# Four batches per attention step, block products in the second MLP matmul, crossbar transposes and list-scheduled engines in a fused retention and MLP kernel

## The chip, the cores and the metric

The kernel runs on one core of one Trainium2 chip. The metric is device time in microseconds (us) of one execution. Each execution was graded fast or slow; on one core slow means over 1.5% above the fastest execution of the same kernel. The medians and ranges quoted hold every execution.

Engine names: PE is the matrix engine (TensorE), PEld its weight load, DVE is VectorE, ACT ScalarE, POOL GpSimd, SP the sequencer that issues most DMAs. "L403" is line 403 of the kernel file, so line numbers belong to one kernel.

## The reference, cut to what matters

```python
# attention: 8 batches, 8 heads, 576 positions, 64 columns a head, no softmax
scores = (1 / 8) * q @ k.transpose                 # per batch and head
gamma  = 1 - 2 ** (-5 - h)
Dmat   = where(i >= j, gamma ** (i - j), 0)
attn   = (scores * Dmat) @ v
x      = attn as (4608 tokens, 512)
# MLP
h = x @ w_in                                       # 512 -> 2048
g = h * cos(h)
out = g @ w_out                                    # 2048 -> 512
```

Both kernels factor the decay into q and v, and work through each sequence in nine chunks of 64 positions with a running 64x64 state per batch and head. The MLP runs in nine blocks of 512 tokens.

Of the kernel before, what the change touches and what calls it, by code (L numbers as in the profile page):

```python
# [14 lines left out]
CH = 64  # L15
NR = S // CH
NST = (B // 2) * NR
# [5 lines left out]
class Op:  # L23
    __slots__ = ("eng", "fn", "deps", "need", "val", "sem", "snap")
# [6 lines left out]
class Prog:  # L31
# [28 lines left out]
    def emit(self):  # L60
# [13 lines left out]
        for op in self.ops:  # L74
# [14 lines left out]
            inst = op.fn(self.handle[op.eng])  # L89
            op.snap = dict(mine)  # L90
# [11 lines left out]

class Kernel:
    def __init__(self, nc, es, q, k, v, w_in, w_out, out):
# [5 lines left out]
        self.NSTG, self.NNAT, self.NKT, self.NQ, self.NPT, self.NSB, self.NCB, self.NOS = 8, 5, 3, 3, 2, 2, 3, 4  # L110
        self.XT = sb("xt", [128, NST * 512], BF16)
        self.WIN = sb("win", [128, 4 * DFF], BF16)
        self.WOUT = sb("wout", [128, NF * DM], BF16)
        self.STG = [sb(f"stg{i}", [128, 2 * DM], F32) for i in range(self.NSTG)]
        self.NAT = [sb(f"nat{i}", [128, 2 * DM], BF16) for i in range(self.NNAT)]
        self.KT = [sb(f"kt{i}", [128, DM], BF16) for i in range(self.NKT)]
        self.QSTG = [sb(f"qstg{i}", [128, 2 * DM], F32) for i in range(self.NQ)]
        self.QNAT = [sb(f"qnat{i}", [128, 2 * DM], BF16) for i in range(self.NQ)]
        self.QT = [sb(f"qt{i}", [128, 2 * DM], BF16) for i in range(self.NQ)]
        self.PT = [sb(f"pt{i}", [128, 512], BF16) for i in range(self.NPT)]  # L120
        self.SBD = [sb(f"sbd{i}", [128, 512], BF16) for i in range(self.NSB)]
        self.GT = [sb(f"gt{i}", [128, NF * TB], BF16) for i in range(2)]
        self.CB = [sb(f"cb{i}", [128, TB], BF16) for i in range(self.NCB)]
        self.OS = [sb(f"os{i}", [128, DM], F32) for i in range(self.NOS)]
# [5 lines left out]
        self.DUM = sb("dum", [128, 512], BF16)  # L130
# [6 lines left out]
        self.SC = nc.alloc_psum_tensor("sc", [128, 1024], F32)  # L137
        self.ST = nc.alloc_psum_tensor("st", [128, 512], F32)
        self.BK = [nc.alloc_psum_tensor(f"bk{i}", [128, 512], F32) for i in range(5)]
        self.held, self.turn = {0}, 0  # L140
        self.n_cb = self.n_os = 0

    def build(self):
        self.constants()
        self.schedule()
        last = self.P.emit()
        for name, val in last.items():
            if name.startswith("o"):
                self.nc.sync.wait_ge(self.P.sems[name], val)


    def constants(self):
        P = self.P
        lng = [math.log(1.0 - 2.0 ** (-5.0 - h)) for h in range(H)]
        P.add("pool", lambda e: e.iota(self.IV.ap(), [[64, 9], [0, 8]], base=0, channel_multiplier=1,
# [4 lines left out]
                                       channel_multiplier=1, allow_small_or_imprecise_dtypes=True), w=["iqx"])  # L160
        for t, key, off, n, sub in ((self.IV, "iv", 0, 72, 64), (self.IQ, "iq", 0, 64, 128),
                                    (self.IQ, "iqx", 64, 8, 64)):
            P.add("dve", lambda e, t=t, off=off, n=n, sub=sub: e.tensor_scalar(
                ap(t, 72, 64, 64, off, [1, n]), ap(t, 72, 64, 64, off, [1, n]), float(sub), None, ALU.subtract),
                r=[key], w=[key])
        P.add("dve", lambda e: e.memset(self.ONE.ap(), 1.0), w=["one"])
        P.add("dve", lambda e: e.memset(self.DUM.ap(), 0.0), w=["dum"])
        for h in range(H):
            P.add("dve", lambda e, h=h: e.memset(ap(self.LV, 72, 0, 128, h, [8, 9]), -lng[h]), w=[("lv", h)])
            P.add("dve", lambda e, h=h: e.memset(ap(self.LQ, 72, 0, 128, h, [8, 9]), lng[h]), w=[("lq", h)])  # L170
        P.add("dve", lambda e: e.memset(self.CLN.ap(), math.log(1.0 / 8.0)), w=["cln"])
        P.add("dve", lambda e: e.memset(self.CPI.ap(), math.pi / 2), w=["cpi"])
# [7 lines left out]
        P.add("pool", lambda e: e.affine_select(self.IDN.ap(), self.ONE.ap(), pattern=[[1, 128]],  # L180
                                                compare_op=ALU.is_equal, fill=0.0, base=0,
                                                channel_multiplier=-1), r=["one"], w=["idn"])
# [12 lines left out]
    def load_kv(self, g, i, gate=()):  # L195
        p, r = g // NR, g % NR
        slot = g % self.NSTG
        for s in range(2):
            self.P.add("sp", lambda e, s=s: e.dma_start(  # L199
                ap(self.STG[slot], 2 * DM, 64 * s, 64, i * DM, [D, H], [1, D]),  # L200
                bass.AP(self.src[1 + i], ((2 * p + s) * H * S + CH * r) * D, [[D, CH], [S * D, H], [1, D]])),
                r=list(gate), w=[("stg", slot, i, s)], sem=f"i{slot}_{i}_{s}")

    def load_q(self, d, gate=()):
        p, r = d // 5, d % 5
        slot, m = d % self.NQ, (2 if d % 5 < 4 else 1) * D
        for s in range(2):
            self.P.add("sp", lambda e, s=s: e.dma_start(
                ap(self.QSTG[slot], 2 * DM, 64 * s, 64, 0, [m, H], [1, m]),
                bass.AP(self.src[0], ((2 * p + s) * H * S + 128 * r) * D, [[m, 64], [S * D, H], [1, m]])),  # L210
                r=list(gate), w=[("qstg", slot, s)], sem=f"q{slot}_{s}")

    def load_win(self, s, gate=()):
        self.P.add("pool", lambda e: e.dma_start(
            ap(self.WIN, 4 * DFF, 0, 128, s * 512, [DFF, 4], [1, 512]),
            bass.AP(self.w_in, s * 512, [[DFF, 128], [128 * DFF, 4], [1, 512]])),
            r=list(gate), w=[("win", s)], sem=f"wi{s}")

    def load_wout(self, s, gate=()):
        self.P.add("pool", lambda e: e.dma_start(  # L220
            ap(self.WOUT, NF * DM, 0, 128, s * 4 * DM, [DM, 4], [1, DM]),
            bass.AP(self.w_out, s * 4 * 128 * DM, [[DM, 128], [128 * DM, 4], [1, DM]])),
            r=list(gate), w=[("wout", s)], sem=f"wo{s}")


    def copy(self, eng, dst, src, r, w):
        if eng == "act":
            self.P.add(eng, lambda e: e.activation(dst, src, AF.Copy), r=r, w=w)  # L228
        else:
            self.P.add(eng, lambda e: e.tensor_copy(dst, src), r=r, w=w)  # L230

    def cast_k(self, g, eng):
        st, na = g % self.NSTG, g % self.NNAT
        self.copy(eng, ap(self.NAT[na], 2 * DM, 0, 128, 0, [1, DM]), ap(self.STG[st], 2 * DM, 0, 128, 0, [1, DM]),
                  [("stg", st, 0, 0), ("stg", st, 0, 1)], [("nat", na, 0)])

    def cast_v(self, g, eng):
        r, st, na = g % NR, g % self.NSTG, g % self.NNAT
        self.P.add(eng, lambda e: e.tensor_tensor(  # L239
            ap(self.NAT[na], 2 * DM, 0, 128, DM, [D, H], [1, D]),  # L240
            ap(self.STG[st], 2 * DM, 0, 128, DM, [D, H], [1, D]),
            ap(self.WV, 72, 0, 128, 8 * r, [1, H], [0, D]), ALU.mult),
            r=[("stg", st, 1, 0), ("stg", st, 1, 1), "wv"], w=[("nat", na, 1)])

    def cast_q(self, d, engs):
        r, k = d % 5, d % self.NQ
        for x, eng in enumerate(engs[:2 if r < 4 else 1]):
            step = 2 * D if r < 4 else D
            self.P.add(eng, lambda e, x=x, step=step: e.tensor_tensor(  # L249
                ap(self.QNAT[k], 2 * DM, 0, 128, x * DM, [D, H], [1, D]),  # L250
                ap(self.QSTG[k], 2 * DM, 0, 128, x * D, [step, H], [1, D]),
                ap(self.WQ, 72, 0, 128, 16 * r + 8 * x, [1, H], [0, D]), ALU.mult),
                r=[("qstg", k, 0), ("qstg", k, 1), "wq"], w=[("qnat", k, x)])

    def bank(self, hold=False):
        while self.turn % 5 in self.held:
            self.turn += 1
        i = self.turn % 5
        self.turn += 1
        if hold:  # L260
            self.held.add(i)
        return i, self.BK[i], ("bk", i)

    def step_tk(self, g, eng="act"):
        k = g % self.NNAT
        i, ps, key = self.bank()
        tb = ps.ap().bitcast(BF16)

        def mm(e):
            for c in range(4):  # L270
                inst = e.transpose(tb[:, c * 128:c * 128 + 128], ap(self.NAT[k], 2 * DM, 0, 128, 128 * c, [1, 128]),  # L271
                                   self.IDN.ap())
            return inst
# [66 lines left out]
    def session(self, g):  # L340
        r = g % NR
        now, nxt = 0 <= g, g + 1 < NST
        if now:
            i, ob, key = self.bank()
# [258 lines left out]
```

## The kernel before: what the change and the argument touch

An attention step covers one chunk of two batches (36 steps). Its small matmuls are 64x64, two batches side by side on the partitions. Keys and queries are transposed on PE against an identity, and evacuated by ACT:

```python
def step_tk(self, g, eng="act"):
    [...]
    for c in range(4):
        inst = e.transpose(tb[:, c*128:c*128+128], ap(self.NAT[k], ..., 128*c, [1,128]), self.IDN.ap())
    self.P.add("pe", mm, r=[("nat", k, 0), "idn"], w=[key])
    self.copy(eng, self.KT[t].ap(), tb[:, 0:512], [key], [("kt", t)])
```

The second MLP matmul is plain: for each 128 tokens, sixteen 512-column matmuls accumulate in one PSUM bank. Program order, per engine, is written by hand: after each few MLP pieces an attention piece is interleaved.

```python
def schedule(self):
    [...]
    for x in range(4):
        self.load_wout(x)
    at["cast"] = 4
    load_to(8, [("wout", 2)])      # the loads of steps 4 to 7 wait for three quarters of w_out
    cast_to(6)
    self.mlp1(0, 2, 0)
    T(4)                           # transposes of step 4: need the gated loads
    self.session(3)
    for f in (1, 2, 3):
        self.mlp1(0, 2, f)
    [...]
    for j in range(1, NTB):
        mlp = []
        for i in range(16):
            mlp.append(m1(4*(j+1), 4*(j+2), i))
            mlp.append(m2(j, i//4, i%4, ...))
        run(mlp, att_of(4*(j+2), 4*(j+3)))
```

## Time and profile before

| | before |
|---|---|
| time, median of 2 runs | 394.2 us (393.95 to 394.46) |
| span of the profiled run | 389.8 us |
| PE busy | 322.7 us, 83% |
| block of 512 tokens with attention | 35.5 us |
| hole on PE near the start | 25.5 to 48.6 us |
| last matmul to the end | 11.3 us |

The first view is the page of the kernel before. The first two lines are the span and the busy time by engine. The rows of digits cut the span into 40 slices; each digit is a busy share in tenths (9 is 90% or more), and PEclk is the granted clock of PE in tenths of full speed. Then come the instruction queue and the chain of waits by engine.

```profile
span 389.8 us, 8844 instructions
...
PE 322.7 (83%) x3695; PEld 172.4 (44%) x3728; DVE 130.3 (33%) x233; ACT 199.1 (51%) x331; POOL 96.1 (25%) x120
...
PE   5640089989777999899899989998998999999980
...
PEclk9555559999988999999999999999999999999995
DMA  8999992154469935363434444554321011001112
...
q8 instruction: 29, 0.48, 0.5%
...
PE 72%; DMA 10%; SPq 6%; ACT 4%; POOL 2%; issue 2%; DVE 0%; DVEq 0%; ACTq 0%; POOLq 0%
```

PE is the bound: it is busy in nearly every slice from the sixth on, and 72% of the chain of waits lies on it. The two zeros in the PE row are the hole. PE's timeline around the hole (start, duration, engine, line, operation, tiles, count; in brackets the idle time before it and what ended it):

```profile
24.50 1.04 PE L403 MATMUL bk<-xt,win 128*128 128x256 bf16 x4
48.59 1.03 PE L288 MATMUL bk<-idn,qnat 128*128 128x128 bf16 x8 [23.06 <-POOL qnat L249]
```

The first four matmuls of block 0 run at 24.50, and then PE sits for 23 us behind the transposes of step 4, whose query cast waits for a load that is gated on w_out.

### The profile page before, as it was taken

The page shows a single profiled execution, that of the slowest core. Times are in us where ns is not written, and L with a number is a line of the kernel's source. Part 1 is how long each engine was busy: PE and PEld are TensorE (multiplying, and loading weights), DVE is VectorE, ACT ScalarE, POOL GpSimd, SP SyncE. Part 2 cuts the span into 40 slices and gives each one's busy share as a digit, 9 for nine tenths or more (in the row PEclk, how much of TensorE's full clock was granted, in tenths as well). Part 3 has the DMA queues.
Part 4 walks back from the last instruction along what each step waited for, and adds up shares of the span by engine and source line. Part 5 has one row for each costly group of instructions (what it writes and reads, how often), then busy time and mean ns, then how long its engine had stood idle before and what let it go on. Part 6 is the DMA issues. An engine that isn't in the chain of part 4 may idle for free.

```text
span 389.8 us, 8844 instructions
## 1 busy us (share of the span) xinstructions
PE 322.7 (83%) x3695; PEld 172.4 (44%) x3728; DVE 130.3 (33%) x233; ACT 199.1 (51%) x331; POOL 96.1 (25%) x120
## 2 busy tenths in 40 slices
PE   5640089989777999899899989998998999999980
PEld 2420064547544545445454545454554454444450
DVE  3410027115532334244333334333343344243100
ACT  3350057349664566556655656655656555444220
POOL 2450273031327431313233323131312000000000
PEclk9555559999988999999999999999999999999995
DMA  8999992154469935363434444554321011001112
GB/s 157 167 190 202 201 208 38 41 136 108 127 161 197 202 98 132 97 176 101 101 97 122 122 122 101 148 138 118 90 80 31 29 33 50 21 31 35 41 46 70
DMA packets 106439, 42.51 MB, mean 109 GB/s; under 512 B 81184, under 2 KB 101920, under 8 KB 106400
## 3 DMA queue, kind: packets, MB, share of 16 engines
q1 hardware_dynamic: 102176, 37.76, 41.7%
q0 software_dynamic: 4224, 4.19, 6.6%
q8 instruction: 29, 0.48, 0.5%
q14 instruction: 10, 0.08, 0.1%
HBM read 36.70 MB, written 9.44 MB: 118 GB/s over the span
## 4 chain that ended last, share of the span: by engine, by line
PE 72%; DMA 10%; SPq 6%; ACT 4%; POOL 2%; issue 2%; DVE 0%; DVEq 0%; ACTq 0%; POOLq 0%
PE bk L403 31%; PE bk L427 29%; SPq L199 4%; DMA wout<-in_moe_w_out_dram 4%; PE bk L334 4%; PE bk L326 3%; DMA qstg<-in_q_dram 2%; DMA out_dram<-os 2%; PE bk L288 2%; PE bk L271 2%; ACT sbd L228 1%; ACT xt L228 1%; PE sc L308 1%; DMA stg<-in_k_dram 1%; POOL qnat L249 1%
## 5 line engine op out<-in xcount | busy, mean ns | idle before, releaser
L413 DVE TENSOR_TENSOR gt<-bk,cb 128x512 bf16<-128x512 f32 (+1 forms) x164 | 102.2, 627 | 179.8 <-ACT cb L410 175.0
L403 PE MATMUL bk<-xt,win 128*128 128x512 bf16 (+1 forms) x656 | 150.3, 363 | 10.5 <-ACT xt L228 10.3
L410 ACT ACTIVATE cb<-bk,cpi 128x512 bf16<-128x512 f32 (+1 forms) x164 | 103.0, 637 | 79.6 <-PE bk L403 79.5
L427 PE MATMUL bk<-wout,gt 128*128 128x512 bf16 (+1 forms) x561 | 137.3, 373 | 2.4 <-ACT os L441 0.7
L403 PEld LDWEIGHTS bk<-xt,win 128*128 128x128 bf16 x656 | 61.8, 101 | 64.1 <-ACT xt L228 11.2
L427 PEld LDWEIGHTS bk<-wout,gt 128*128 128x128 bf16 x592 | 57.4, 98 | 66.9 <-ACT os L441 2.1
L230 POOL CAST nat<-stg 128x512 bf16<-128x512 f32 x32 | 19.5, 610 | 172.6 <-PE st L316 102.3
L239 POOL TENSOR_TENSOR nat<-stg,wv 128x512 bf16<-128x512 f32 x36 | 37.5, 1042 | 13.0 <-DMA stg<-in_v_dram 12.7
L376 DVE TENSOR_TENSOR pt<-sc,tri 128x512 bf16<-128x512 f32 x36 | 24.6, 683 | 46.0 <-PE sc L308 46.0
L288 PE MATMUL bk<-idn,qnat 128*128 128x128 bf16 x144 | 12.5, 233 | 29.2 <-POOL qnat L249 26.4
L249 POOL TENSOR_TENSOR qnat<-qstg,wq 128x512 bf16<-128x512 f32 x32 | 32.8, 1041 | 11.4 <-DMA qstg<-in_q_dram 11.4
L228 ACT ACTIVATE qt<-bk 128x1024 bf16<-128x1024 bf16 (+1 forms) x18 | 16.7, 928 | 33.4 <-PE bk L288 33.4
L441 ACT ACTIVATE os<-bk 128x512 f32<-128x512 f32 (+1 forms) x37 | 21.7, 585 | 22.3 <-PE bk L427 22.3
L228 ACT ACTIVATE sbd<-st 128x512 bf16<-128x512 f32 x32 | 19.1, 598 | 23.5 <-PE st L316 23.5
L228 ACT ACTIVATE kt<-bk 128x512 bf16<-128x512 bf16 x36 | 21.4, 594 | 12.0 <-PE bk L271 12.0
L334 PE MATMUL bk<-pt,nat 64*64 64x64 bf16 x576 | 23.6, 204 | 3.2 <-PE st L316 0.5
L288 PEld LDWEIGHTS bk<-idn,qnat 128*128 128x128 bf16 x144 | 10.0, 104 | 33.8 <-POOL qnat L249 27.4
L228 ACT ACTIVATE xt<-bk 128x512 bf16<-128x512 f32 x36 | 21.4, 594 | 2.3 <-PE bk L334 2.3
L308 PE MATMUL sc<-qt,kt 64*64 64x64 bf16 x576 | 20.6, 204 | 1.5 <-DVE qt L230 0.8
L316 PE MATMUL st<-nat 64*64 64x64 bf16 x512 | 21.1, 205 | 0.0
L334 PEld LDWEIGHTS bk<-pt,nat 64*64 64x64 bf16 x576 | 15.5, 113 | 8.6 <-PE st L316 6.4
L326 PEld LDWEIGHTS bk<-qt,sbd 64*64 64x64 bf16 x512 | 11.4, 115 | 15.5 <-ACT cb L410 10.3
(36 smaller groups left out, 98.8 us busy)
## 6 DMA issues: line engine op xcount, KB each, us to landing
stg<-in_k_dram SPq DMA_DIRECT2D x72, 128.0 KB, 7.3
stg<-in_v_dram SPq DMA_DIRECT2D x72, 128.0 KB, 4.7
out_dram<-os SPq DMA_DIRECT2D x70, 128.0 KB
qstg<-in_q_dram SPq DMA_DIRECT2D x32, 256.0 KB, 5.9
win<-in_moe_w_in_dram POOLq DMA_DIRECT2D x4, 512.0 KB, 8.0
wout<-in_moe_w_out_dram POOLq DMA_DIRECT2D x4, 512.0 KB, 15.3
qstg<-in_q_dram SPq DMA_DIRECT2D x8, 128.0 KB, 4.5
out_dram<-os SPq DMA_DIRECT2D x4, 64.0 KB
```

The source lines that it names most:

```text
L228: self.P.add(eng, lambda e: e.activation(dst, src, AF.Copy), r=r, w=w)
L239: self.P.add(eng, lambda e: e.tensor_tensor(ap(self.NAT[na], 2 * DM, 0, 128, DM, [D, H], [1, D]), ap(self.STG[st], 2 * DM, 0, 128, DM, [D, ...
L249: self.P.add(eng, lambda e, x=x, step=step: e.tensor_tensor(ap(self.QNAT[k], 2 * DM, 0, 128, x * DM, [D, H], [1, D]), ap(self.QSTG[k], 2 * ...
L288: inst = e.transpose(tb[:, o:o + 128], ap(self.QNAT[k], 2 * DM, 0, 128, x * DM + 128 * c, [1, 128]), self.IDN.ap())
L308: yield lambda c=c: e.matmul(ap(self.SC, 1024, 64 * s, 64, hp * 512 + c * 64, [1, 64]), ap(kt, DM, 64 * hp, 64, c * 128 + 64 * s, [1, 64]) ...
L326: yield lambda c=c, s=s: e.matmul(ap(ob, 512, 64 * hp, 64, c * 128 + 64 * s, [1, 64]), ap(sbd, 512, 64 * hp, 64, s * 256 + c * 64, [1, 64] ...
L334: yield lambda c=c: e.matmul(ap(ob, 512, 64 * hp, 64, c * 128 + 64 * s, [1, 64]), ap(na, 2 * DM, 64 * s, 64, DM + (2 * c + hp) * D, [1, D] ...
L376: self.P.add("dve", lambda e: e.tensor_tensor(ap(self.PT[pt], 512, 0, 128, 0, [256, 2], [64, 4], [1, 64]), ap(self.SC, 1024, 0, 128, 0, [5 ...
L403: inst = e.matmul(ap(ps, 512, 0, 128, 0, [1, n]), ap(self.WIN, 4 * DFF, 0, 128, c * DFF + 128 * f, [1, 128]), ap(self.XT, NST * 512, 0, 12 ...
L410: self.P.add("act", lambda e: e.activation(ap(cb, TB, 0, 128, 0, [1, n]), ap(ps, 512, 0, 128, 0, [1, n]), AF.Sin, bias=self.CPI.ap(), scal ...
L413: self.P.add("dve", lambda e: e.tensor_tensor(ap(gt, NF * TB, 0, 128, f * TB + off, [1, n]), ap(ps, 512, 0, 128, 0, [1, n]), ap(cb, TB, 0, ...
L427: return e.matmul(ap(ps, 512, 0, 128, 0, [1, cn]), ap(gt, NF * TB, 0, 128, f * TB + 128 * t, [1, 128]), ap(self.WOUT, NF * DM, 0, 128, f * ...
```

## The change

Its intent: shorten PE's work (fewer small matmul slots, fewer columns in the second MLP matmul, no transposes), and fill the start. It has five parts.

1. A step covers four batches (18 steps). Scores, state update, inter-chunk and intra-chunk products run on the four 64x64 quarters of the array in turn.
2. In blocks 1 to 8 the second MLP matmul is done as seven block products (a Strassen-Winograd form) of 256 columns, with sums of the left operand on DVE, and sums of w_out made once. Block 0 stays plain.
3. Keys and queries are transposed by the DMA crossbar from step 4 on.
4. A list scheduler, given a duration for every task, fixes each engine's order.
5. The first half of block 0 comes before the inputs of step 3, and stores cover two batches at once.

The diff is 1154 lines long; this is its core, with cuts marked.

```diff
-        load_to(8, [("wout", 2)])
-        self.mlp1(0, 2, 0)
-        T(4)
-        self.session(3)
[...]
+    FORDER = [0, 1, 2, 3, 8, 9, 10, 11, 4, 5, 6, 7, 12, 13, 14, 15]
+    GATE = {2: [("wout", 1, 0)], 3: [("wout", 3, 0)]}
+    PLAIN = (0,)
+    XBAR = 4
[...]
+        if u < self.XBAR:
+            self.tpe(z["natk"], ...)              # transpose on PE, as before
+        else:
+            self.txb(z["natk"], ..., "tk", 2600)  # 2.6 us is the scheduler's duration
[...]
+    def txb(self, src, rk, n, dst, wk, sem, work):
+        self.one("sp", 700, lambda e: e.dma_start_transpose(
+            ap(self.at(dst), 1024, 0, 128, 0, [128, n], [1, 128]),
+            ap(self.at(src), 1024, 0, 128, 0, [1, 128 * n])), ...)
[...]
+    def wino2(self, j, base, span):
+        # S1 = A21 + A22; S2 = S1 - A11; S3 = A11 - A21; S4 = A12 - S2, each in two halves, on DVE
+        for q in range(2):
+            [...] self.one("dve", 610, lambda e, ...: e.tensor_tensor(sv(i, q), x(), y(), op), ...)
+        for n, p in enumerate((1, 2, 6, 5, 7, 3, 4)):    # seven products, 16 matmuls of 256 columns each
+            l, rr, keys, bank, first = spec[p]
+            for q in range(2):
+                self.one("pe", 8 * 109, mm, r=keys(q), w=[(bank,)], prio=..., name=f"P{p}_{j}")
[...]
+        for j in range(NTB):
+            if j == 1:
+                self.wsums()                             # sums of w_out, once
+            [...]
+            if j in self.PLAIN:
+                self.plain2(j, base, PER)
+            else:
+                self.wino2(j, base + 900, 12200 if last else PER)
```

## The prediction

> **What bounds it now.** TensorE (PE). The table of busy time gives PE 322.7 of 389.8 us; in 10 us windows between 125 and 365 us PE is 86 to 99% busy at clock 1.00. The chain of waits lies 72% on PE, 31% on the first and 29% on the second MLP matmul. In the timeline, four 512-column matmuls start every 0.864 us (216 ns each), so 128 of them make 27.7 us a block of 512 tokens. The chain shows a block with attention repeating every 35.5 us: about 7.8 us are attention, transposes and small stalls. PE does almost nothing from 25.5 to 48.6 us (in program order behind a query load gated on w_out), loses about 6 us near 112 to 118 us (another query load, after an SP backlog), and the kernel ends 11.3 us after the last matmul, in stores that take about 9 us to land.
>
> **What changes, per block of 512 tokens (PE).**
> - Seven block products: 112 matmuls of 256 columns for 64 of 512. The 256-column tail runs at about 113 ns, the 512 ones at 216: 12.2 to 12.7 us for 13.8. Saves about 1.4 us, eight blocks: 11 us.
> - Attention: a step for two batches takes 1.15 us now (131.25 to 132.40). Slots of four quarters start about 31 ns apart; 40 slots serve four batches, so about 1.6 us for 2.3. Saves 1.4 us a block, 12 us in all.
> - Transposes by DMA from step 4: 224 of 288 PE transposes (56 ns, plus waits) go, 14 us, with their ACT evacuations.
> - Adds on DVE: eight bf16 sums and four combinations a block, about 7.5 us; DVE then has some 21 of 29 us, ACT 18, POOL 11.
> - Adds on DMA: 224 tiles of 32 KB. [...]the kernel's own scheduler assumes 2.6 us, with which DMA needs some 25 us of a block: tight, not binding.
>
> New block: 13.8 + 12.4 + 3.1, about 29 us.
>
> **Start and end.** Loads before the weights take 17 us and the weights until 40 us in both kernels. The new order lets block 0's first matmul (and most of its second) run while weights land, so about 15 us of the 23 us hole is filled; inputs of steps 2 to 5 still arrive late, leaving some 10 us of stalls by 78 us. By then blocks 0 and 1 should be nearly done. Left: seven blocks of MLP, 7 x 26.2 = 184, and steps 18 us: 280. Plus about 12 us for banks (six, a step needs four) and order misfits, and 5 to 8 us of tail[...]: about 300 us.
>
> **Prediction:** 300 us, 285 to 320. Chances: faster by over 2% 0.97, within 2% 0.015, slower 0.015.
>
> **What would show it right.** PE matmuls fall by about 12% of dense columns in the second MLP part; block period 29 to 31 us; the hole at 25 to 49 us mostly gone; transposes on the DMA queue landing in under 5 us; last store landing within 6 us of the last matmul; clock 1.00 in mid-run.
>
> **What would make it wrong.** Crossbar transposes far slower than 2.6 us or blocking the other loads (DMA share near 1, PE waiting on the transposed keys): 320 to 350. A fixed order from wrong durations, with SP stores holding back loads: PE stalls at each step. DVE's bf16 sums at half the assumed rate. A tighter start: 285 or less.

How the sum is made: 78 us for the start, 184 + 18 us for seven blocks and their steps (280), 12 us of misfits and 5 to 8 us of tail come to about 300 us. "Tight, not binding" was the estimate from the 2.6 us per transposing DMA that the scheduler in the kernel's source assumes. The trace of the kernel after has these numbers for terms that were estimates: 8.3 us of DVE sums and combinations a block for 7.5 (the 64 half sums took 0.78 us each, the 24 combinations 0.68 us); in a block without gaps (155.8 to 184.3 us) DVE busy for 20.9 us, ACT 16.8, POOL 10.2; stores landing 3.3 us after their issue in the median (2.4 to 5.0), where the chain of the kernel before has one of 9.15 us. What the transposes cost is under a_xbar18.

## The result, and the profile after

The kernel after takes 325.03 us (324.32 to 325.75, 2 runs), correct, against 394.2 us. The ratio of the two is 0.8245, with a 95% interval of 0.8164 to 0.8327. Ratios here and below are the mean time of one kernel's fast runs over that of the other's in the same rounds, so they are not quite the ratio of the medians quoted. The direction was predicted; the time lies 5 us above the top of the predicted range and 25 us above its centre.

The page of the kernel after, with the lines that answer to those shown of before:

```profile
span 324.0 us, 9377 instructions
...
PE 288.4 (89%) x3925; PEld 195.7 (60%) x3925; DVE 196.7 (61%) x324; ACT 170.8 (53%) x282; POOL 102.8 (32%) x120
...
PE   6749999696878995998999999999995999999994
...
PEclk9766999789999997899999999999999799999999
DMA  7999999889979999995699998998895200220135
...
q1 hardware_dynamic: 126976, 43.53, 68.8%
...
q8 instruction: 31, 0.51, 0.7%
...
PE 78%; DVE 6%; issue 6%; ACT 4%; DMA 2%; POOL 2%; ACTq 1%; DVEq 0%; POOLq 0%
```

Three things differ from what was expected. The PE row has dips (6, 6, 8, 7 and 8) from slice 8 to slice 13, that is 57 to 105 us, and a 5 in slice 16 and in slice 31 (122 to 130 and 243 to 251 us). PEclk falls to 7 or 8 in those places or just behind them. And "issue", time in which the engine waited for nothing that the profile shows, has grown from 2% to 6% of the chain.

PE's timeline after, at the first matmul of block 0, at the first matmul of block 2, and in the middle of two attention steps:

```profile
24.99 1.03 PE L654 MATMUL bk<-xt,win 128*128 128x512 bf16 x2 [1.42 <-ACT xt L430]
...
62.32 6.35 PE L654 MATMUL bk<-xt,win 128*128 128x256 bf16 x36 [1.41 <-ACT xt L430]
...
87.53 1.04 PE L776 MATMUL bk<-tw,s 128*128 128x256 bf16 x8
...
93.73 1.92 PE L776 MATMUL bk<-tw,s 128*128 128x256 bf16 x16 [1.82 <-DVE s L737]
...
103.96 4.28 PE L654 MATMUL bk<-xt,win 128*128 128x512 bf16 x19 [1.42 <-ACT xt L430]
...
126.16 0.26 PE L546 MATMUL st<-natv,natk 64*64 64x64 bf16 x2 [3.49 <-issue]
126.17 0.68 PE L563 MATMUL bk<-pt,natv 64*64 64x64 bf16 x18
126.78 1.89 PE L776 MATMUL bk<-tw,s 128*128 128x256 bf16 x8
...
251.06 0.19 PE L563 MATMUL bk<-pt,natv 64*64 64x64 bf16 x1 [3.34 <-issue]
```

Block 1 starts at 62.32 us and block 2 only at 103.96 us; the prediction had put the equivalent point at 78 us. At 126.16 and 251.06 PE resumes a step after 3.5 and 3.3 us in which no semaphore held it: 108 and 107 of the 128 small matmuls had already been issued without a pause. After the first of these gaps, eight 256-column matmuls take 1.89 us where eight of the same form took 1.04 us at 87.53: PE is back at half its clock (granted 0.50 from 126 to 130 us). Behind the second gap the granted clock was 0.66 from 252 to 256 us. How long a gap has to be for that, the runs do not settle: 2.26 us in a_m30 was followed by half clock (0.50 from 128.8 to 132.2 us), 2.69 us in a_w3 was not (1.00 from 163 to 175 us).

To see where PE's time goes I worked out, from the trace, the spacing from each matmul's start to the next one's, and took off the spacing that the same shape has back to back in dense stretches (216 ns at 512 columns, 109 at 256, 56 at 128, and up to 15 for one of the small matmuls of a step). What is taken off is called work here, the remainder lost. For the kernel after, with no matmul record missing:

| stretch | us | work | lost |
|---|---|---|---|
| start to first MLP matmul | 25.0 | | |
| first MLP matmul to first matmul of block 2 | 79.0 | 59.8 | 19.2 |
| block 2's first matmul to the last matmul | 215.8 | 192.8 | 22.7 |
| last matmul to the end | 4.3 | | |

Where no gap falls, the blocks from block 2 on repeat every 28.4 us: stores at 155.8, 184.3 and 212.6 us. With both gaps the mean from the first matmul of block 2 (103.96 us) to that of block 8 (282.20 us) is 29.7 us.

### The profile page after: what moved, and what is told of

It reads as the page before. It is cut to its first block, busy times and chain, and to the rows that moved or that the text cites. A ratio compares the mean times of both kernels' runs of the same rounds, so it can differ in the third digit from the quotient of the medians.

```text
span 324.0 us, 9377 instructions
## 1 busy us (share of the span) xinstructions
PE 288.4 (89%) x3925; PEld 195.7 (60%) x3925; DVE 196.7 (61%) x324; ACT 170.8 (53%) x282; POOL 102.8 (32%) x120
## 4 chain that ended last, share of the span: by engine, by line
PE 78%; DVE 6%; issue 6%; ACT 4%; DMA 2%; POOL 2%; ACTq 1%; DVEq 0%; POOLq 0%
PE bk L654 38%; PE bk L776 28%; PE bk L690 4%; DVE gt L665 3%; PE bk L555 3%; DMA stgk<-in_k_dram 2%; PE bk L563 2%; DVE s L737 2%; ACT xt L430 2%; PE st L546 2%; PE bk L538 1%; POOL natv L473 1%; DVE s L743 1%; ACTq L423 1%; ACT cb L662 1%
## 5 line engine op out<-in xcount | busy, mean ns | idle before, releaser
L468 POOL TENSOR_TENSOR qnat<-stgq,wq 128x512 bf16<-128x512 f32 x32 | 36.4, 1161 | 43.8 <-DMA stgq<-in_q_dram 38.9
L473 POOL TENSOR_TENSOR natv<-stgv,wv 128x512 bf16<-128x512 f32 x36 | 39.0, 1091 | 35.1 <-DMA stgv<-in_v_dram 35.0
L431 POOL CAST natk<-stgk 128x512 bf16<-128x512 f32 x32 | 19.8, 629 | 52.6 <-DMA stgk<-in_k_dram 32.8
L776 PE MATMUL bk<-tw,s 128*128 128x256 bf16 x256 | 32.9, 277 | 1.8 <-DVE s L737 1.8
L776 PE MATMUL bk<-wout,gt 128*128 128x256 bf16 x256 | 33.1, 276 | 1.1 <-DVE gt L665 1.1
L776 PE MATMUL bk<-wout,s 128*128 128x256 bf16 x256 | 31.7, 273 | 0.0
L776 PEld LDWEIGHTS bk<-tw,s 128*128 128x128 bf16 x256 | 25.2, 99 | 9.4 <-DVE s L737 2.1
L614 DVE TENSOR_TENSOR pt<-bk,tri 128x512 bf16<-128x512 f32 x36 | 23.1, 683 | 12.5 <-PE bk L538 12.5
L776 PEld LDWEIGHTS bk<-wout,gt 128*128 128x128 bf16 x256 | 25.3, 99 | 8.4 <-DVE gt L665 1.4
L776 PEld LDWEIGHTS bk<-wout,s 128*128 128x128 bf16 x256 | 24.6, 98 | 6.9
L430 ACT ACTIVATE os<-bk 128x512 f32<-128x512 f32 x12 | 7.2, 601 | 19.8 <-PE bk L776 10.6
```

The source lines that it names most:

```text
L430: return self.one(eng, dur, lambda e: e.activation(dst(), src(), AF.Copy), r=r, w=w, **kw)
L431: return self.one(eng, dur, lambda e: e.tensor_copy(dst(), src()), r=r, w=w, port=True, **kw)
L468: self.one(qe, 620 if qe == "dve" else 990, lambda e, tt=tt, x=x, step=step: e.tensor_tensor(ap(self.at(z["qnat", tt]), 1024, 0, 128, x * ...
L473: self.one(ve, 990, lambda e, tt=tt: e.tensor_tensor(ap(self.at(z["natv"]), 1024, 0, 128, 512 * tt, [D, H], [1, D]), ap(self.at(z["stgv"]) ...
L614: self.one("dve", 610, lambda e, hp=hp: e.tensor_tensor(ap(self.at(y["pt"]), 1024, 0, 128, 512 * hp, [64, 8], [1, 64]), ap(self.at(y["sc"] ...
L776: inst = e.matmul(ap(self.at(bank), 512, 0, 128, 256 * tt, [1, 256]), l(f, tt), rr(f), start=(first and f == 0 and tt == 0), stop=True, sk ...
```

## The experiments

The kernel before took between 391.6 and 393.0 us (medians) in the four groups of runs; each ratio uses its own group. All runs gave a correct result, except one. Two things to keep in mind: lengths of gaps are from here on taken by the accounting above (start to start, less the shape's spacing), which makes them about 0.2 us longer than the idle time in the profile's brackets; and every edit of the new kernel except a_wide and the shifts also makes the list scheduler order all engines anew, so order changes with it. Two theories stood at the outset. Theory A: the DMA engines, whose row is close to full until about 245 us, hold PE up. Theory B: PE is held by order and by its own issue, at the start and in the gaps.

### a_wide: the same bytes of q, k and v in longer runs (wrong result)

```diff
-                bass.AP(self.src[src], at + s*H*S*D, [[m, 64], [S*D, H], [1, m]])),
+                bass.AP(self.src[src], at + s*H*S*D, [[m*H, 64], [1, m*H]])),
```

> Same bytes of q, k and v, read as one contiguous run per partition (2 or 4 KB instead of 8 runs of 256 or 512 B), so the result is wrong on purpose; the order on every engine is unchanged. Theory A (the start is late because the DMA engines are saturated, so the inputs of steps 0 to 5 land late): the first inputs land by about 10 us instead of 17, the stores of block 1 come about 15 us earlier than 131.9, and the time falls by 10 to 20 us to 305 to 315. Theory B (fixed order[...] stall PE, not DMA): within 4 us of 325.

Measured: 322.25 us, ratio 0.8232 (0.8176 to 0.8288); the unaltered kernel had 0.8245 at first and 0.8299 in a_again below, with 325.03 and 326.06 us, so 3 to 4 us are gained by the medians and less by the ratios. The DMA share fell from 0.90 to 0.71 in the window 105 to 160 us and from 1.00 to 0.84 in 160 to 240 us. PE's lost time fell in the first 30 us (18.1 to 13.0 us: the inputs of the first steps arrive sooner) and hardly anywhere else; time waited for semaphores after 30 us was 16.6 us against 16.0. Both gaps inside steps remained (2.85 and 3.25 us, after the same 108 and 107 matmuls). Theory A falls for all but the first 25 us. A reserve: the edit leaves the number of DMAs that SP issues as it was.

### a_xbar18 and a_xbar8: transposes back on PE

```diff
-    XBAR = 4
+    XBAR = 18      # a_xbar18: no crossbar transpose at all;  a_xbar8: XBAR = 8
```

> All transposes back on PE (288 instead of 64), DMA loses 224 tiles, about 73 us of 16-engine time. If DMA saturation cost as much as the transposes saved, the time stays within 4 us of 325 (theory A with the transposes as its cause). If DMA was not what held PE (theory B), PE gets 224 x 56 ns = 12.5 us plus evacuations on ACT: 337 to 345.

> Transposes of steps 4 to 7 back on PE too (64 more, 3.6 us of PE), which takes 21 us of 16-engine time off DMA before about 110 us. Theory A: block 1 is done earlier and the time falls by 4 to 10 us. Theory B: up by 2 to 5 us.

Measured: a_xbar18 332.64 us, ratio 0.8464 (0.8407 to 0.8521); a_xbar8 325.78 us, 0.8332 (0.8280 to 0.8383). Without the crossbar PE's work rises by 12.0 us (260.5 to 272.5), close to the 14 us of the prediction, but the time rises by only about 7 us (against 325.03 and 326.06 us), and a fifth of the kernel's DMA time goes away: its 16 engines are busy for an estimated 62.7% of 330.9 = 207 us instead of 80.7% of 324.0 = 261 us. So 224 transposes of 32 KB cost an estimated 54 us of DMA time in this mix, 1.9 us for 256 KB; the 73 us expected were 28 times the scheduler's 2.6 us. The time of a_xbar18 lies between what the two theories had set (within 4 us of 325, and 337 to 345), so it decides for neither. The first four crossbar steps (a_xbar8) are worth nothing measurable.

### a_shift14 and a_m30: the same schedule, the instruction stream moved

These add 14 warm-up matmuls at the very start, or take 30 away, and touch nothing else. A matmul is two instructions in the stream, a weight load and a product (3925 records of each in the kernel after).

```diff
-                    self.warm(int((gap - 300) // 110))
+                    self.warm(int((gap - 300) // 110) + (14 if warm == 0.0 else 0))   # a_shift14
+                    self.warm(int((gap - 300) // 110) - (30 if warm == 0.0 else 0))   # a_m30
```

> 14 more warm-up matmuls (28 instructions) in idle time before the first real work; nothing else. Theory F (the two 3.5 us gaps inside attention steps at 122.5 and 247.5 us, which no semaphore explains, come from where the step lies in PE's instruction stream): those two gaps vanish or move to other steps, and the time falls by up to 7 us if they vanish. Rival (the gaps come from a late data wait or from DMA at that moment): they stay at the same steps and the time is within 1 us of 325.

> 30 fewer of the first 51 warm-up matmuls, which moves every later PE instruction 60 places forward in its stream. Theory F (PE runs dry of fetched instructions at stream positions 193 or 194 of every 256 when a step follows closely on another): that position now falls near the start (10 matmuls in) of the two steps that stalled, both gaps vanish with the cold clock that follows them, and the time falls by 5 to 10 us. Rival (other steps then stall instead[...]): as many gaps elsewhere and no gain.

Measured: a_shift14 327.31 us, 0.8362 (0.8312 to 0.8412). Its gaps came after 94 and 93 matmuls of the step instead of 108 and 107, at 126.44 and 249.70 us: exactly 14 matmuls earlier in the step, so at the same position in the instruction stream (instructions 3266 and 6849, both 193 or 194 past a multiple of 256). a_m30: 324.13 us, 0.8200 (0.8141 to 0.8259). The two old gaps were gone, but three new ones that no semaphore ended stood in dense stretches at 59.8 us (again inside a step), 124.9 and 248.3 us (1.4, 2.4 and 2.6 us). So the rival of its expectation, gaps elsewhere and no gain, came closer: against a_again in the same group it is 2 us faster by the medians, with intervals that overlap. PE's timeline of a_shift14 at the first gap:

```profile
126.43 0.20 PE L546 MATMUL st<-natv,natk 64*64 64x64 bf16 x2
129.01 0.26 PE L563 MATMUL bk<-pt,natv 64*64 64x64 bf16 x2 [2.38 <-issue]
```

What is fetched there can be read from the trace too. The instruction queue (q8) brings packets of 16 KB; in the kernel after 31 of them serve 7991 weight loads, matmuls and waits in PE's stream, 258 for each packet; a packet takes 0.9 to 1.9 us. In the kernel after, one such packet runs from 123.59 to 124.93 us, inside the gap, and PE resumes 1.23 us after it. Over all fourteen runs with the new structure there are 32 gaps of at least 1.4 us after the first 30 us that no semaphore ends; 30 of them, 1.4 to 4.9 us long, end 1.2 to 1.7 us after the landing of such a packet. Counted in the traces, these 30 all begin 193 to 195 instructions past a multiple of 256. The other two, in a_plain9 and a_w3, begin 38 and 37 past one, at the first matmul of a step, and end 0.1 us after the step's transposed keys landed (145.94 and 144.33 us): they are waits for keys that the profile did not name, and are counted as such below. So the reading is that at the 30 PE runs out of instructions; it rests on this agreement of positions and landings. The kernel before has no such gap of 0.8 us or more, nor has b_start below; in the kernel before the packets after 60 us are never closer than 7.6 us, while in the kernel after they come as close as 3.6 us. What makes a given packet late is not settled: before both gaps in the kernel after it started 5.4 to 5.5 us after PE had passed the like position of the previous 256 instructions, where no other packet of that run after the first 30 us started more than 3.4 us after it; and a_w2 below passes such a position at the same place in a step with no gap.

### a_again: the unaltered kernel once more, five rounds

> The changed kernel once more, unaltered, as the yardstick for the other runs of this job: 323 to 327 us, with gaps of about 3.5 us inside the attention steps at about 122 and 247 us.

Measured: 326.06 us (323.82 to 328.19), 0.8299 (0.8252 to 0.8346). Gaps of 3.96 and 3.77 us in the same two places. This is the base for the runs below.

### a_plain9: no seven-product form anywhere

```diff
-    PLAIN = (0,)
+    PLAIN = tuple(range(NTB))      # and no sums of w_out
```

> The second MLP matmul as 64 plain matmuls of 512 columns in all blocks, no block sums on DVE. If PE work sets the pace from block 1 on: 8 x (13.8 - 12.4) = 11 us slower. If the sums on DVE[...] and the banks they hold cost PE as much as they save: within 4 us of the changed kernel.

Measured: 328.65 us, 0.8363 (0.8317 to 0.8409), so 2.5 us slower than a_again by the ratios, with intervals that overlap. PE's work is an estimated 273.3 us (267.0 in the records, plus 29 records of 512 columns that are missing from this trace), 13 us more than in a_again. So the form does save PE the predicted work, 1.6 us a block; but 10.5 us of it is given back. The waits tell a good part of where: PE waited for semaphores for 9.6 us after the first 30 us, against 16.2 us in a_again. From the first MLP matmul to block 2 it needs 72.0 us, against 78.7 us.

### a_w2: block 1 also plain

If what is lost at 50 to 105 us is that the seven-product form of block 1 has nothing to offer while the inputs of steps 3 to 5 are late, then plain products there, which go half a block at a time, should fill it.

```diff
-    PLAIN = (0,)
+    PLAIN = (0, 1)
-            if j == 1:
+            if j == 2:
                 self.wsums()
```

> Blocks 0 and 1 plain, so the eight weight sums on DVE (8.3 us, between 80 and 95 us) come a block later, and the sums of block 1 go. If DVE is what holds PE between 60 and 105 us (theory B): 3 to 6 us faster, after 1.4 us more PE work. If not: 0 to 2 us slower.

Measured: 310.40 us (309.40 to 312.34), 0.7906 (0.7859 to 0.7953), faster than the kernel after by 15 us. One reason in the expectation was wrong: the sums of w_out ran at about 40 to 54 us in the kernel after, where DVE was idle, not at 80 to 95 us. Three of the windows, for a_again and then for a_w2 (columns: window, length, busy time and count of PE, PEld, DVE, ACT and POOL, granted clock, DMA share, GB/s):

```profile
60.00:105.00 45.00, 35.87 (x682) 29.19 (x679) 27.01 (x51) 25.12 (x52) 19.68 (x22) 0.93 1.04 184
105.00:160.00 55.00, 49.30 (x704) 30.44 (x702) 39.27 (x58) 31.72 (x51) 22.80 (x24) 0.94 0.93 176
160.00:240.00 80.00, 78.40 (x1234) 53.39 (x1232) 56.87 (x84) 46.42 (x76) 31.62 (x35) 1.00 0.96 191
```

```profile
60.00:105.00 45.00, 39.31 (x717) 26.38 (x723) 23.37 (x49) 28.50 (x58) 19.15 (x23) 1.00 1.03 191
105.00:160.00 55.00, 51.55 (x640) 32.64 (x631) 42.02 (x61) 33.63 (x53) 24.33 (x26) 1.00 0.97 192
160.00:240.00 80.00, 78.65 (x1356) 54.08 (x1354) 57.49 (x85) 47.43 (x79) 32.94 (x36) 1.00 0.98 193
```

PE is busier before 160 us and never falls from its full clock, at the same DMA share; from 160 us on the windows are alike. Block 2 starts at 96.10 us. But the gaps without a semaphore were nearly gone as well (1.4 and 1.0 us), so this run alone could not tell how much of the 15 us was the filled stretch, and how much was luck.

### b_start: the start of the change, alone, in the kernel before

```diff
         cast_to(6)
-        self.mlp1(0, 2, 0)
+        for f in range(16):
+            self.mlp1(0, 2, f)
         T(4)
         self.session(3)
-        for f in (1, 2, 3):
-            self.mlp1(0, 2, f)
-        for f in range(4):
-            self.mlp1(2, 4, f)
-        for f in range(4, 16):
-            self.mlp1(0, 4, f)
+        for f in range(16):
+            self.mlp1(2, 4, f)
```

> The kernel before with one part of the change alone: all sixteen first matmuls of the first half block (64 of 256 columns, about 7 us) go into PE's program ahead of the query transposes that wait behind w_out, instead of four of them. If the 23 us hole at 25 to 49 us was an ordering fault: 4 to 6 us faster than before (6 us of work moves into the hole). If those matmuls only wait for w_in there: within 2 us.

Measured: 387.18 us, 0.9873 (0.9843 to 0.9904), so 5 us faster, as expected. Of the 23 us hole, a reordering of half of block 0's first matmul recovers 5. What fills the rest was not tested apart; in the kernel after, where two four-batch steps give the whole of block 0 its input, PE loses 2.0 us between 25 and 49 us, against 23.6 us before.

### b_xbar2: the crossbar transposes alone, in the kernel before

```diff
 def step_tk(self, g, eng="act"):
+        if g >= 8:
+            self.P.add("sp", lambda e: e.dma_start_transpose(
+                ap(self.KT[t], DM, 0, 128, 0, [128, 4], [1, 128]), ap(self.NAT[k], ...)), ..., sem=f"tk{t}")
+            return
[...]                                # the same for the queries from their fifth tile on
```

A first form, with two DMAs a query tile, was refused before it ran, for a race on the tile; this one has one.

> The kernel before with crossbar transposes alone, from its step 8 on (the same 224 of 288 tiles). The prediction's term: 12.5 us of PE and its ACT copies go, and DMA has room (48% busy): 10 to 15 us faster. Rival (the transposes stand in the SP queue behind casts and hold back the loads): less than 5 us faster, or slower.

Measured: 444.13 us, 1.1323 (1.1283 to 1.1363): 52 us slower, where 10 to 15 us faster was expected. PE's work fell by an estimated 12 us, as it should, and the waits took all of it back. Waits of PE and then of SP's queue (what waits, for what, total us, times, longest):

```profile
PE bk L340 <- DMA kt<-nat: 50.8, 14, 16.8
PE bk L300 <- POOL qnat L249: 23.7, 1, 23.7
```

```profile
SPq L460 <- ACT os L455: 72.5, 15, 14.6
SPq L199 <- DMA wout<-in_moe_w_out_dram: 24.9, 1, 24.9
```

PE waits 50.8 us for transposed keys, while SP stands for 72.5 us, in 15 waits, at stores whose data ACT has not written yet; transposes placed behind those stores in SP's program come late with them. The transposes need an order on SP that knows when things are ready. So the parts of the change do not add: the crossbar is worth about 7 us with the list scheduler and costs 52 us in the hand-written order.

### a_w2v: a_w2, with the value casts of the first two steps on DVE

```diff
-            ke, qe, ve = ("act", "dve", "pool") if early else ("pool", "pool", "pool")
+            ke, qe, ve = ("act", "dve", "dve") if early else ("pool", "pool", "pool")
```

> The version with blocks 0 and 1 plain (310.4 us), and the v casts of steps 0 and 1 on DVE instead of Pool. Those casts ended two PE waits of about 2 us each before the first MLP matmul: 2 to 3 us faster than 310, if nothing else is late there.

Measured: 309.72 us (307.09 to 310.42), 0.7882 (0.7840 to 0.7923). Within the noise of a_w2, and the fastest of all versions; it beats both kernels.

### a_w2x8: a_w2, with transposes of steps 4 to 7 on PE

> Blocks 0 and 1 plain and transposes of steps 4 to 7 on PE (3.6 us of PE work). If steps 4 to 7 are late because of DMA and the SP queue, block 2 starts earlier than 96 us and the time is 2 to 6 us under 310. If not: 3 to 5 us over it.

The edit is a_w2 with `XBAR = 8`. Measured: 324.57 us, 0.8283 (0.8242 to 0.8324). It gives back nearly the whole gain of a_w2, although PE's work rises by an estimated 3.6 us only (263.4 against 260.7 in the records, and ten against six missing ones), and the DMA share in 60 to 105 us falls from 1.03 to 0.83. The gaps without a semaphore add up to 13.4 us, the most of any run: 2.7, 2.9, 1.6, 2.4, 1.9 and 1.9 us from 69 us on. Three of the six lie in that relieved stretch, so a lower load on the DMA engines did not make them rarer here, and a crowded DMA is not their cause by itself.

### a_w2p14, a_w2m30 and a_w3: is the gain of a_w2 the filled stretch or luck in where the gaps fall?

The first two are a_w2 with the shifts of a_shift14 and a_m30. The third has `PLAIN = (0, 1, 2)`, with the sums of w_out made at block 3.

> Block 1 in plain products, plus 14 extra warm-up matmuls at the start, which move the instruction stream by 28 instructions. Theory of the missing filler: block 2 still starts at about 96 to 97 us and the time stays at 309 to 314 us. Rival[...]: semaphore-less gaps of 3 to 4 us come back inside attention steps and the time rises by 5 to 10 us, to 315 to 320.

> Block 1 in plain products, with 30 warm-up matmuls fewer (60 instructions). Theory of the missing filler: 307 to 313 us, block 2 starting at 95 to 97 us. Rival[...]: 315 to 320 us with one or two gaps of 2 to 4 us that no semaphore ends.

> Blocks 0, 1 and 2 in plain products. If the starved stretch ends with block 1, as the filler theory has it, block 2 gains nothing from plain products and pays the 1.4 us that the seven-product form saves: 311 to 313 us against 310.4. If the lateness of inputs reaches into block 2 (to about 125 us), this run is as fast or faster: 306 to 310.

Measured: a_w2p14 318.35 us, 0.8119 (0.8073 to 0.8165); a_w2m30 319.22 us, 0.8140 (0.8085 to 0.8194); a_w3 315.31 us, 0.8062 (0.8012 to 0.8113). The rival got its number: shifts that change no work but the warm-up cost 8 to 9 us. PE's timeline of a_w2p14, at the start of block 2 and at its longest gap, then of a_w2m30 at one of its two:

```profile
97.18 5.35 PE L654 MATMUL bk<-xt,win 128*128 128x512 bf16 x24 [1.42 <-ACT xt L430]
...
118.12 0.83 PE L776 MATMUL bk<-wout,gt 128*128 128x256 bf16 x6
123.17 0.61 PE L776 MATMUL bk<-wout,gt 128*128 128x256 bf16 x2 [4.21 <-issue]
```

```profile
76.28 0.60 PE L690 MATMUL bk<-wout,gt 128*128 128x512 bf16 x2
79.73 2.74 PE L690 MATMUL bk<-wout,gt 128*128 128x512 bf16 x6 [2.85 <-issue]
```

Block 2 still starts at 97.18 us in a_w2p14; the gap comes later, in the middle of eight equal MLP matmuls, right behind a step. In a_w2m30 a gap at 76.5 us falls into the filled stretch itself, and block 2 starts at 102.65 us.

The same accounting of PE's time for the runs that matter, after the first 30 us (gaps of at least 0.3 us, by what ended them; "rest" holds half-clock stretches and small change; a_w2 and a_w2v lack six matmul records, about 1.3 us, which appear in their rest):

| run | median us | ratio to before | waits for semaphores | gaps without semaphore | rest |
|---|---|---|---|---|---|
| a_again (as after) | 326.06 | 0.8299 | 16.2 | 8.6 | 17.0 |
| a_plain9 | 328.65 | 0.8363 | 9.6 | 8.6 | 16.7 |
| a_w2p14 | 318.35 | 0.8119 | 8.5 | 9.5 | 11.9 |
| a_w2m30 | 319.22 | 0.8140 | 9.7 | 7.8 | 14.1 |
| a_w3 | 315.31 | 0.8062 | 8.6 | 6.1 | 9.4 |
| a_w2 | 310.40 | 0.7906 | 11.2 | 2.8 | 10.5 |
| a_w2v | 309.72 | 0.7882 | 7.4 | 3.0 | 10.6 |

The row of a_plain9 holds missing records too, so its rest is too high by about 6 us. The table separates the two effects. Every version in it with block 1 in plain products waits 5 to 9 us less for semaphores than a_again: this is the edit's own gain. The stretch from the first MLP matmul to the first of block 2 says the same: 79.0 and 78.7 us in the kernel after and a_again, 70.6 to 72.3 us in five of the seven runs with block 1 plain, though their orders differ; the two others (77.4 us in a_w2m30, 77.6 us in a_w2x8) have gaps without a semaphore of 3.0 and 7.2 us in it. In the two shifted runs, whose gaps are like those of a_again, it is (0.8299 - 0.8119) x 392 = 7 us and (0.8299 - 0.8140) x 392 = 6 us of time. The rest of a_w2's gain, some 8 us, is that its gaps happen to be short: 2.8 us instead of 7.8 to 9.5, and less half-clock time behind them. a_w3 is 3 to 4 us faster than the two shifted runs, but its interval overlaps theirs and its gaps are 2 to 3 us shorter, so it does not show whether the starved stretch reaches into block 2.

## Why the prediction was wrong, point by point

**Right, in part by luck: the steady part.** The prediction had 202 us of matmul work left after its point "blocks 0 and 1 nearly done", plus 12 us of misfits and 5 to 8 us of tail, 219 to 222 us. From the first matmul of block 2 the trace shows 192.8 us of work, 22.7 us lost and 4.3 us of tail, 220 us. About 6 us of the loss is spacing of over 15 ns inside steps, which the prediction had in its steps; so compared, work is 199 us for 202, losses 17 us for 12 and tail 4.3 us for 5 to 8. The losses hold 7.8 us of gaps that nothing in the prediction foresaw, and smaller terms elsewhere made up for them: the total is closer than its reasons. The period is 28.4 us without a gap and 29.7 us with them (predicted 29 to 31), a four-batch step takes about 1.5 us from 100.91 us (predicted 1.6), transposes land after 4.1 to 4.2 us in the median (predicted below 5), and the last store lands 4 us after the last matmul (predicted within 6).

**Wrong, and the step that failed:** "inputs of steps 2 to 5 still arrive late, leaving some 10 us of stalls by 78 us. By then blocks 0 and 1 should be nearly done." The point came at 103.96 us, 26 us later, which is the whole miss of 25 us. The term was mis-sized twice. First, the work: from the first MLP matmul at 24.99 us to block 2 PE had 59.8 us of work, where 78 - 25 - 10 leaves room for 43. So 17 us of the miss is a sum that I never did; 25 + 60 = 85 us was the earliest possible time with no stall at all. The text counted the hole as filled by 15 us, and then counted the blocks as done as well. The hole itself is nearly gone, as said under b_start. Second, the stalls: 19.2 us instead of 10.

**What made the stalls:** a_w2 and its shifted forms show that 5 to 9 us of waiting is due to block 1's seven-product form. The reading is that most of it has nothing to run until both halves of the block and the DVE sums exist, at the time when the inputs of steps 3 to 5 set the pace; the runs show the edit's effect, and this reason for it is argued from the dependencies. The prediction costed that form by its PE work alone. a_plain9 shows the same from the other side: 13 us of work saved by the form in all blocks, 2.5 us of time gained.

**Not foreseen: running out of instructions.** Gaps that no semaphore ends, 7.8 us in the kernel after and 8.6 us in a_again, plus half-clock time behind the longer ones, are in the new structure; the old one has none of 0.8 us or more. They were hidden in "clock 1.00 in mid-run", which the profile contradicts: PEclk shows 7 or 8 in three stretches. The shift runs and the positions in the stream (30 of 30) show where PE can stop; whether it stops there varies. The same two shifts cost a_w2 8 to 9 us, but moved the kernel after by only about 1 us up and 2 us down. That PE waits for its instructions there is read from the packets (the 30 gaps end 1.2 to 1.7 us after one landed); what makes a packet late is open.

**Partly right: DMA "tight, not binding".** The 7.3 MB of transposes cost an estimated 54 us of 16 engines' time, 136 GB/s, and 256 KB landed in 4.1 to 4.2 us in the median. Even so the DMA share near 1 was not what held PE: a_wide took it down to 0.71 to 0.84 with the waits unchanged, and won 3 to 4 us by the medians; PE's lost time fell by 5.1 us in the first 30 us.

**Partly right: transposes.** Predicted 14 us off PE; measured 12 us of work, about 7 us of time.

## What to carry to other kernels

When a change rewrites the start, add up the work that must be done before the steady part and compare it with the time you allow; a point on the time axis is a sum too. A cheaper algorithm that needs its whole input before it starts can lose on a starved stretch what it saves elsewhere, so use it where the pipeline is full and keep the finer-grained form where inputs are late. When time is lost in front of an instruction that waited for nothing, move the instruction stream by some no-effect instructions and run again before crediting or blaming any edit: here such shifts alone cost a_w2 8 to 9 us, and moved the kernel after by 1 to 2 us.
